# One attention-and-MoE kernel: the first unit's work in one written order, constants in one block, keys in blocks of 32

## The chip, the cores and the metric

The kernel runs on one core of a Trainium2 chip. The metric is the device time of one execution in microseconds (us); the kernel before takes 814.76 us (median of 3 runs, 812.94 to 815.05).

A core has a matrix engine (TensorE: PE for the multiplications, PEld for the loading of their stationary operand), a vector engine (VectorE, DVE), an activation engine (ScalarE, ACT), GpSimd (POOL) and SyncE (SP). Each engine works through its own queue in order and waits on semaphores of the others. Transfers (DMA) are issued from the queue of SP or POOL.

## What is computed

Three layers follow each other, on 2304 tokens (batch 4, sequence 576, 8 heads of 64):

```python
scores = scale * np.matmul(q, k.transpose(0, 1, 3, 2))
rel = pos[:, None] - pos[None, :]
mask_plain = (rel >= 0) & (rel < 32)                      # heads 0 to 3
mask_dil = (rel >= 0) & (rel < 128) & (rel % 4 == 0)      # heads 4 to 7
scores = np.where(mask, scores, -1e9)
attn = np.exp(scores - scores.max(-1)); attn = attn / (attn.sum(-1) + 1e-9)
x = attn @ v                                              # 2304 x 512
h = np.maximum(np.maximum(x @ w1, x @ w2), x @ w3)        # d_ff 768
x = h @ w_out                                             # 2304 x 512
h = x @ w_in                                              # d_ff 2048
g = (a0 + a1*h + a2*h*h + a3*h*h*h) / (1 + |b0|*|h| + |b1|*h*h + 1e-6)
out = g @ w_out2
```

The weights arrive as 64-bit floats.

## The kernel before

**Stages.** The attention and the first MoE are worked through in 6 units of 384 tokens; a unit has 2 chunks of 192 tokens (chunks 0 to 11, three to a batch). Behind the last unit the second MoE runs over 6 tiles of 384 tokens (from about 420 us on).

**Attention of a chunk** has a plain half `p` (heads 0 to 3) and a dilated half `d` (heads 4 to 7). Its steps are: `S` scores (PE, lines 278 and 287; in chunks 0 to 3 PE adds the mask as a product with an identity), `MX` row maximum (DVE, line 307), `E` exponential (ACT, line 318, one instruction a block with a sum in chunks 0 to 3, one for all blocks behind them), `SB` division by the sum (DVE, lines 328 to 330), `X` transposes (PE, line 343) with a copy out of PSUM (ACT line 347 or DVE line 345), `V` product with the values (PE, lines 363 and 369), `VE` the split of the result into a rounded high part `x1h` (ACT, line 384) and a low part `x1l` (DVE, line 385).

**First MoE of a unit** (`moe1`): 18 groups of 12 matmuls of 384 columns (lines 497 to 499: high by high, high by low, low by high), each group's result copied by ACT (line 514) or joined by DVE's maximum (line 516), with a split of the maximum (lines 520, 521), then 4 groups of 18 matmuls whose results go to DRAM (`x2d`) by POOL's queue (line 531).

**Weights of the first MoE** are 18 blocks `w1r` and 6 blocks of `w_out` of 512 KB. Each takes five steps: `load` (SP), `abs` (ACT, line 450), `bits` (two on DVE, lines 456 and 458), `hi` (ACT, line 472), `lo` (DVE, line 480). The second MoE's weights are converted later and stored as `w2d` by POOL's queue (line 478), at a pace tied to PE's progress.

**Order.** The text `START` is a list of words that is issued exactly as written: chunks 0 and 1, a few conversion steps, and `W:n`, n matmuls of 512 columns whose result nobody reads (`warmth`, line 604). Behind it a scheduler of the language orders the instructions by data and priority: unit 0's `moe1` with the conversions and the attention of chunks 2 and 3 (`UNIT0`), then each later unit's `moe1` with the attention of the next (`UNIT`). Loads of queries, keys and values stand on SP's queue.

Of the kernel before, what the change touches and what calls it, by code (L numbers as in the profile page):

```python
# [31 lines left out]

START = """
W:7
S0:p v:0 L:3 S0:d MX0:p E0:p MX0:d S1:p W:2
SB0:p E0:d X0:p,0,1 X0:p,1,1 W:1 MX1:p V0:p SB0:d abs VE0:p bits E1:p S1:d abs X0:d,0,1 W:2 MX1:d X0:d,1,1 W:3 V0:d E1:d W:2 SB1:p VE0:d hi abs lo v:1 L:3
X1:p,0 W:2 SB1:d X1:p,1 bits W:3 V1:p hi W:2 VE1:p lo bits
X1:d,0 W:2 X1:d,1 W:3 V1:d VE1:d hi lo abs
"""

UNIT0 = """
Sa:p
MXa:p Ea:p SBa:p
-
Xa:p,1 Sa:d MXa:d Ea:d SBa:d
-
-
Xa:p,0 Va:p Xa:d,0
VEa:p Xa:d,1
-  # L50
Va:d
VEa:d
-
Sb:p
MXb:p Eb:p
Sb:d MXb:d SBb:p Eb:d Xb:p,0
SBb:d Xb:p,1 Xb:d,0
-
Xb:d,1 Vb:d Vb:p VEb:d
VEb:p  # L60
-
-
-
# [29 lines left out]
def kernel(  # L93
    ctx: ExitStack,
    tc: tile.TileContext,
    masks: bass.AP,
# [10 lines left out]
    a_co: bass.AP,  # L107
    b_co: bass.AP,
# [40 lines left out]
    AHEAD = 1  # L149
# [38 lines left out]
    at_k = {}  # L188
    x1 = {}

    def load_k(b, part=None):

        if b not in at_k:
            at_k[b] = (
                at.tile([128, 2, S], F32, tag="kTp", bufs=2, name=f"kTp{b}"),
                at.tile([128, 8, S // 4], F32, tag="kTd", bufs=2, name=f"kTd{b}"),
            )
        kTp, kTd = at_k[b]
        src = kp_in[b].rearrange("p (a t) -> p a t", a=2)
        if part is None:  # L200
            nc.sync.dma_start(out=kTp, in_=src)
        elif part == 0:
            nc.sync.dma_start(out=kTp[:, :, 0:CH], in_=src[:, :, 0:CH])
            return
        else:
            nc.sync.dma_start(out=kTp[:, :, CH:S], in_=src[:, :, CH:S])
            return
        nc.sync.dma_start(out=kTd.rearrange("p n m -> p (n m)"), in_=kd_in[b])

    def load_q(c, g):  # L210
        if c >= NCH:
            return
        if g == "p":
            t = at.tile([128, 2 * BP, 2 * QP], F32, tag="qTp", bufs=QA, name=f"qTp{c}")
            nc.sync.dma_start(out=t.rearrange("p n w -> p (n w)"), in_=qp_in[c])
        else:
            t = at.tile([128, 8, 2 * M], F32, tag="qTd", bufs=QA, name=f"qTd{c}")
            nc.sync.dma_start(out=t.rearrange("p n w -> p (n w)"), in_=qd_in[c])
        at_raw[c, g] = t
# [8 lines left out]
    def load_v(c):  # L228
        ci = c % NC
        vp = at.tile([WP, BP, NP, D], F32, tag="vp", name=f"vp{c}")  # L230
        nc.sync.dma_start(out=vp.rearrange("p i h d -> p (i h d)"), in_=vp_in[c])
        nm = dil(ci)[1]
        vd = at.tile([WD, NP, 4 * D], F32, tag="vd", name=f"vd{c}")
        nc.sync.dma_start(out=vd[:nm].rearrange("p h e -> p (h e)"), in_=vd_in[c, 0:nm, :])
        at_raw[c, "v"] = (vp, vd)

    def attn_pieces(c):
# [12 lines left out]
        def SC(g):  # L250
# [6 lines left out]
            for j in range(2):  # L257
                at_bank = SC_AT.get((c, g), "sc")
                if at_bank != "sc":
                    t = (mm_p if at_bank == "mm" else pv_p).tile(  # L260
                        [128, 512], F32, tag=at_bank, name="sc")
                else:
                    t = sc_p.tile([128, 512], F32, tag="sc", bufs=2, name="sc")
# [11 lines left out]
            m16, m32 = (mP16, mP32) if plain else (mD16, mD32)  # L275
# [4 lines left out]
            for n in range(U):  # L280
                i, blk = divmod(n, BP)
                if plain:
                    k0 = key0(ci, blk)
                    lq, rk = qT[:, n, :], kTp[:, i, k0:k0 + WP]
                else:
                    lq, rk = qT[:, n, :], kTd[:, n, m0:m0 + nmk]
                nc.tensor.matmul(scs[n // G][:, n % G, :], lhsT=lq, rhs=rk,  # L287
                                 start=not pem, stop=not pem or n % G == G - 1)
            load_q(c + QA, g)
            if g == "d" and ci == 0 and b + 1 < B:  # L290
                load_k(b + 1)
            sb = at.tile([Q, U, WP if plain else WD], F32, tag="s" + g, bufs=SBB, name="sb")
            mx = at.tile([Q, U, 1], F32, tag="mx" + g, bufs=2, name="mx")
            sm = at.tile([Q, U, 1], F32, tag="sm" + g, bufs=2, name="sm")
            grp[g] = (sb[:, :, :W], Q, W, U, sm, mx, scs, mask(m32))

        def MX(g):
# [11 lines left out]
            if c < ACT_UNITS:  # L309
                nc.vector.tensor_scalar_mul(mx, mx, -SCALE)  # L310

        def E(g):
            sv, Q, W, U, sm, mx, scs, mk = grp[g]
            G = U // 2
            if c < ACT_UNITS:
                for n in range(U):
                    src = scs[n // G][:, n % G, :] if c < MASK_PE else sv[:, n]
                    nc.scalar.activation(out=sv[:, n], in_=src, func=AF.Exp, scale=SCALE,
                                         bias=mx[:, n], accum_out=sm[:, n])
            else:  # L320
                nc.vector.tensor_tensor(out=sv, in0=sv, in1=mx.to_broadcast([Q, U, W]),
                                        op=ALU.subtract)
# [3 lines left out]
        def SB(g):  # L326
# [3 lines left out]
            nc.vector.tensor_tensor(out=sv, in0=sv, in1=sm.to_broadcast([Q, U, W]), op=ALU.mult)  # L330

        def X(g, j, dve=False, bank="tp"):
            sv, Q, W, U = grp[g][:4]
            G = U // 2
            if bank == "tp":
                tp = tp_p.tile([128, TU], F32, tag="tp", name="tpp")
            else:
                tp = sc_p.tile([128, 512], F32, tag="sc", bufs=2, name="tpp")[:, 0:TU]
            tp = tp[:W].rearrange("w (n q) -> w n q", q=Q)
            pt = at.tile([WP, TU], F32, tag="pt", bufs=PT, name="pt")[:W].rearrange(  # L340
                "w (n q) -> w n q", q=Q)
# [8 lines left out]
        def V(g):  # L350
            vp, vd = at_raw[c, "v"]
            if c == 0:
                pv = mm_p.tile([128, 512], F32, tag="mm", name="pv")
            else:
                pv = pv_p.tile([128, 512], F32, tag="pv", name="pv")
            pv = pv[:, 0:TU].rearrange("p (a t) -> p a t", a=2)
            for a in range(2):
                pt = pts["p", a] if g == "p" else None
                for n in range(BP if g == "p" else 4):
                    for j in range(2):  # L360
# [6 lines left out]
                        else:  # L367
                            pt = pts["d", j]
                            nc.tensor.matmul(pv[rows, a, M * n:M * n + M],  # L369
                                             lhsT=vd[:nmk, 2 * a + j, D * n:D * n + D],  # L370
                                             rhs=pt[:, 2 * (n // 2) + a,
                                                    M * (n % 2):M * (n % 2) + M],
# [3 lines left out]
        def VE(g):  # L376
            pv = grp["v" + g]
            if g == "p":
                src, dh, dl = pv, x1h[:, 0:2, tok], x1l[:, 0:2, tok]
            else:  # L380
# [65 lines left out]
    def cv_abs(i):  # L446
# [27 lines left out]
    def cv_lo(i):  # L474
# [4 lines left out]
        else:  # L479
            nc.vector.tensor_sub(slot[:, 512:1024], t, slot[:, 0:512].bitcast(F32))  # L480

    cv_at = {"load": 0, "abs": 0, "bits": 0, "hi": 0, "lo": 0}
    cv_steps = (("hi", cv_hi, "bits"), ("lo", cv_lo, "bits"), ("abs", cv_abs, "load"),
                ("bits", cv_bits, "abs"), ("load", cv_load, None))

# [15 lines left out]

    def moe1(u):
        x1h, x1l = x1[u]
        hs = {}
        for f in range(F1):
            for j in range(3):
                ps = mm_p.tile([128, 512], F32, tag="mm", name="mm")
                o = ps[:, 0:TU]
                w = w1s[f, j]
                mm3(o, [(w[:, 128 * c:128 * c + 128], w[:, 512 + 128 * c:640 + 128 * c],  # L510
                         x1h[:, c, :], x1l[:, c, :]) for c in range(KC)])
                if j == 0:
                    t = com.tile([128, TU], F32, tag="m", bufs=MB, name="m")
                    nc.scalar.activation(out=t, in_=o, func=AF.Copy)
                else:
                    nc.vector.tensor_tensor(out=t, in0=o, in1=t, op=ALU.max)  # L516
                if j == 2:
                    hh = com.tile([128, TU], F32R, tag=f"hh{f}", name=f"hh{f}")
# [386 lines left out]
```

## Time and profile before

| | us |
|---|---|
| median of 3 runs | 814.76 |
| the profiled execution | 815.14 |
| its span, first to last instruction | 813.4 |

The profile was taken from one execution. Its page gives busy times and the chain of work that ended last; its trace can be asked for stretches, single lines, tiles and rows in order of time. Times in rows are counted from the span's start. A busy PE is not PE at its peak: matmuls overlap, so the pace is read from start to start. PEclk is the granted TensorE clock, 1.00 for 2.4 GHz and 0.50 for 1.2 GHz.

### The profile page before, as it was taken

To read this page: it belongs to the slowest core of one execution; us is meant where nothing else is said; L and a number is where in the kernel's file an instruction comes from. 1 tells how busy PE (TensorE), PEld (TensorE's weight loads), DVE (VectorE), ACT (ScalarE), POOL (GpSimd) and SP (SyncE) were. 2 spreads that over 40 slices of the span, in tenths; PEclk is the share of its full clock that TensorE was granted. 3 is DMA by queue.
4 is the path that set the end of the run, shared out by engine and by line. 5 is a ranking of instruction groups with operands and counts; after the bars stand their busy time and mean duration, and the time that the engine had idled before them with its cause. 6 is when DMAs were issued, how large, how long until landed. Compare 5 with 4: busy or idle time off the path is not lost.

```text
span 813.4 us, 13081 instructions
## 1 busy us (share of the span) xinstructions
PE 800.1 (98%) x4965; PEld 745.1 (92%) x4965; DVE 614.1 (76%) x1184; ACT 487.9 (60%) x1023; POOL 39.2 (5%) x77
## 2 busy tenths in 40 slices
PE   7899999999999999999999999999999999999998
PEld 5699999999999999999998899999999999999996
DVE  2679755655656646637389899999999999998996
ACT  3578623333333334245398887787778778777775
POOL 0000000110111110000000000000000000000000
PEclk9799999999999999999999999999999999999999
DMA  8677435754554544328310011010002001001001
GB/s 267 245 263 271 159 106 171 228 167 158 171 175 161 178 163 149 107 101 272 120 63 1 1 39 40 1 42 37 1 1 79 1 0 40 1 1 38 2 1 39
DMA packets 29438, 82.54 MB, mean 101 GB/s; under 512 B 3904, under 2 KB 7488, under 8 KB 29376
## 3 DMA queue, kind: packets, MB, share of 16 engines
q1 hardware_dynamic: 24080, 64.66, 24.7%
q0 software_dynamic: 5296, 17.04, 5.5%
q8 instruction: 39, 0.64, 0.3%
q14 instruction: 23, 0.19, 0.1%
HBM read 63.87 MB, written 17.83 MB: 100 GB/s over the span
## 4 chain that ended last, share of the span: by engine, by line
PE 96%; ACT 1%; DVE 1%; DMA 1%; issue 0%; SPq 0%; POOL 0%; ACTq 0%
PE mm L498 12%; PE mm L497 12%; PE mm L499 12%; PE h L498 8%; PE acc L769 8%; PE h L499 8%; PE h L497 8%; PE acc L767 8%; PE acc L768 8%; PE sc L287 4%; PE tpp L343 2%; PE pv L369 2%; PE pv L363 1%; DMA mk<-in_masks_dram 1%; ACT x1h L384 1%; PE warmth L604 0%
## 5 line engine op out<-in xcount | busy, mean ns | idle before, releaser
L497 PE MATMUL mm<-x1h,w1s 128*128 128x384 f32 x432 | 147.7, 343 | 0.0
L498 PE MATMUL mm<-x1l,w1s 128*128 128x384 f32 x432 | 146.0, 338 | 1.0 <-DVE x1l L385 1.0
L499 PE MATMUL mm<-x1h,w1s 128*128 128x384 f32 x432 | 145.2, 336 | 0.0
L498 PE MATMUL h<-x2l,w2s 128*128 128x384 f32 x384 | 129.2, 337 | 0.0
L499 PE MATMUL h<-x2h,w2s 128*128 128x384 f32 x384 | 129.0, 336 | 0.0
L497 PE MATMUL h<-x2h,w2s 128*128 128x384 f32 x384 | 128.9, 336 | 0.0
L767 PE MATMUL acc<-w2s,gh 128*128 128x512 f32 x288 | 113.6, 395 | 0.0
L768 PE MATMUL acc<-w2s,gh 128*128 128x512 f32 x288 | 113.4, 394 | 0.0
L769 PE MATMUL acc<-w2s,gl 128*128 128x512 f32 x288 | 109.8, 395 | 0.0
L718 ACT ACTIVATE q<-h 128x384 f32<-128x384 f32 x96 | 47.2, 491 | 76.1 <-PE h L499 75.5
L498 PEld LDWEIGHTS mm<-x1l,w1s 128*128 128x128 f32 x432 | 81.6, 189 | 2.2 <-DVE x1l L385 2.2
L497 PEld LDWEIGHTS mm<-x1h,w1s 128*128 128x128 f32 x432 | 81.3, 189 | 0.6
L499 PEld LDWEIGHTS mm<-x1h,w1s 128*128 128x128 f32 x432 | 81.6, 189 | 0.0
L497 PEld LDWEIGHTS h<-x2h,w2s 128*128 128x128 f32 x384 | 72.1, 188 | 3.9
L498 PEld LDWEIGHTS h<-x2l,w2s 128*128 128x128 f32 x384 | 72.0, 188 | 3.8
L499 PEld LDWEIGHTS h<-x2h,w2s 128*128 128x128 f32 x384 | 72.1, 188 | 0.3
L516 DVE TENSOR_TENSOR m<-mm,m 128x384 f32<-128x384 f32 x72 | 39.9, 554 | 42.2 <-PE mm L499 41.4
L725 DVE SCALAR_TENSOR_TENSOR q<-q,cs,ab 128x384 f32<-128x384 f32 x96 | 59.1, 615 | 15.5 <-ACT ab L719 15.4
L720 ACT ACTIVATE p<-h,cs 128x384 f32<-128x384 f32 x96 | 65.1, 678 | 0.0
L769 PEld LDWEIGHTS acc<-w2s,gl 128*128 128x128 f32 x288 | 54.1, 188 | 11.9
L768 PEld LDWEIGHTS acc<-w2s,gh 128*128 128x128 f32 x288 | 54.1, 188 | 9.4
L767 PEld LDWEIGHTS acc<-w2s,gh 128*128 128x128 f32 x288 | 54.0, 188 | 9.0
(86 smaller groups left out, 1471.8 us busy)
## 6 DMA issues: line engine op xcount, KB each, us to landing
w1r<-in_w_dram SPq DMA_DIRECT2D x18, 512.0 KB, 6.6
raw<-in_w_in_dram SPq DMA_DIRECT2D x16, 512.0 KB, 4.0
w2d<-cvt POOLq DMA_DIRECT2D x32, 256.0 KB, 2.6
raw<-in_w_out_dram SPq DMA_DIRECT2D x16, 512.0 KB, 3.6
w2r<-w2d SPq DMA_DIRECT2D x32, 256.0 KB, 3.6
qTp<-in_qp_dram SPq DMA_DIRECT2D x12, 384.0 KB, 4.1
qTd<-in_qd_dram SPq DMA_DIRECT2D x12, 384.0 KB, 4.5
x2d<-xs POOLq DMA_DIRECT2D x24, 192.0 KB, 2.5
```

The lines of the kernel that those rows point to most:

```text
L287: nc.tensor.matmul(scs[n // G][:, n % G, :], lhsT=lq, rhs=rk, start=not pem, stop=not pem or n % G == G - 1)
L343: nc.tensor.transpose(tp[:, i, :], sv[:, G * j + i, :], ident[:Q, :Q])
L497: nc.tensor.matmul(o, lhsT=lh, rhs=rh, start=(i == 0), stop=False)
L498: nc.tensor.matmul(o, lhsT=lh, rhs=rl, start=False, stop=False)
L499: pe_at[0] = nc.tensor.matmul(o, lhsT=ll, rhs=rh, start=False, stop=(i == n - 1))
L516: nc.vector.tensor_tensor(out=t, in0=o, in1=t, op=ALU.max)
L718: nc.scalar.activation(out=s["q"], in_=s["h"], func=AF.Square)
L720: nc.scalar.activation(out=s["p"], in_=s["h"], func=AF.Identity, scale=cs[:, 3:4], bias=cs[:, 2:3])
L725: nc.vector.scalar_tensor_tensor(out=s["q"], in0=s["q"], scalar=cs[:, 5:6], in1=s["ab"], op0=ALU.mult, op1=ALU.add)
L767: nc.tensor.matmul(o, lhsT=gh, rhs=w[:, 0:512], start=(c == 0), stop=False)
L768: nc.tensor.matmul(o, lhsT=gh, rhs=w[:, 512:1024], start=False, stop=False)
L769: nc.tensor.matmul(o, lhsT=gl, rhs=w[:, 0:512], start=False, stop=(c == F2 - 1))
```

## The change

The written order `START` now holds all of unit 0: the attention of chunks 0 to 3, all 24 weight conversions and all of unit 0's `moe1`, so that the scheduler begins with unit 1's `moe1`. The word for the conversion's first step is now `up`. New words: `H:j` is group j of `moe1` on the first 192 columns, `P:n` group n on the rest or on all columns, `M`, `HH`, `HL`, `Y`, `YS` the steps behind a group. `W:n` no longer issues matmuls of 512 columns but 4n of 128 columns, in the bank that the next step takes. `E` is one of three kinds in chunks 0 to 3 (`A` with sums by ACT, `C` block by block with the sum by DVE, `B` one instruction for all blocks), and the division may be done by ACT (`SB0:p,act`).

The two masks and the identity come in 16 bits in the same block as the coefficients (`consts`), so that two casts and the two small coefficient loads go. Plain keys lie in blocks of 32 tokens, first the one half of the heads, then the other. The tokens of a chunk are ordered by their rest modulo 4 within 64, and the host puts the output's rows back; so the split of a dilated result reads and writes rows without a stride, and the `V` matmul of the dilated half writes three runs of 16. Loads of queries, keys and values behind the start go to POOL's queue.

```diff
-W:7
-S0:p v:0 L:3 S0:d MX0:p E0:p MX0:d S1:p W:2
...
+qp0 kp0 mk L W:19 S0:p,mm qd0 kd0 up MX0:p bits L E0:p qd1 hi W:10 S0:d,mm SM0:p L up lo
+SB0:p,act MX0:d W:1 S1:d,sc qp1 D0:d bits kp1 E0:d X0:p,0,mm up X0:p,1,mm SM0:d v0 XC0:p,0 MX1:d
...
+    EXPS = {"0:p": "C", "1:d": "A", "2:p": "A", "2:d": "A", "3:p": "C", "3:d": "C"}
...
+    def keep_warm(t):
+        for _ in range(4 * idle[0]):
+            nc.tensor.matmul(t[:, 384:512], lhsT=warm, rhs=warm, start=True, stop=True)
+        idle[0] = 0
+        return t
...
+        queue = nc.sync if b < 2 else nc.gpsimd        # load_k
+        queue = nc.sync if c < 2 * QA else nc.gpsimd   # load_q
+        queue = nc.sync if c < 4 else nc.gpsimd        # load_v
...
-                    lq, rk = qT[:, n, :], kTp[:, i, k0:k0 + WP]
+                    lq, rk = qT[:, n, :], kTp[:, k0 // 32:(k0 + WP) // 32, i, :]
...
-                            nc.tensor.matmul(pv[rows, a, M * n:M * n + M],
-                                             lhsT=vd[:nmk, 2 * a + j, D * n:D * n + D],
+                            at_n = pv[rows, a].rearrange("p (i r m) -> p r i m", r=4, m=16)[:, n]
+                            nc.tensor.matmul(at_n, lhsT=vd[:nmk, 2 * a + j, D * n:D * n + D],
...
-                src = pv.rearrange("p a (r m) -> p a r m", r=4)
-                dh = x1h[:, 2:4, tok].rearrange("p a (m r) -> p a r m", r=4)
-                dl = x1l[:, 2:4, tok].rearrange("p a (m r) -> p a r m", r=4)
+            return pv, x1h[:, at_p, tok], x1l[:, at_p, tok]
...
+                elif op == "H":
+                    m1_mm(0, 0, int(arg), slice(0, CH))
+                elif op == "P":
+                    f, j = divmod(int(arg), 3)
+                    m1_mm(0, f, j, slice(CH if (0, f, j) in m1 else 0, TU))
...
-        for u in range(NU):
+        for u in range(1, NU):
```

What stood on PE ahead of the first group of `moe1` before: an unread matmul, the last `V` of chunk 1, then three matmuls of 384 columns that repeat with the next weights.

```order
L604 LDWEIGHTS warm
L604 MATMUL warmth<-warm 128x512
L369 MATMUL pv<-pt,vd_389 64x48 x16
L497 MATMUL mm<-x1h_172,w1s_0_382 128x384
L498 MATMUL mm<-x1l_173,w1s_0_382 128x384
L499 MATMUL mm<-x1h_172,w1s_0_382 128x384
```

And on PE now (`vd_373` and `vd_421` are the values of chunks 0 and 1, `spare` holds chunk 1's probabilities):

```order
L376 MATMUL tpp<-mk,spare 80x96 x8
L407 MATMUL pv<-pt,vd_373 64x3x16 x16
L407 MATMUL pv<-pt,vd_421 64x3x16 x16
L376 MATMUL tpp<-mk,spare 96x128 x6
L537 MATMUL mm<-x1h_150,w1s_0_261 128x192
L538 MATMUL mm<-x1l_151,w1s_0_261 128x192
L539 MATMUL mm<-x1h_150,w1s_0_261 128x192
```

The first group now stands ahead of chunk 1's plain `V`, on 192 columns, without an unread matmul near it.

DVE at the start of the program before (L307 maximum, L328 to L330 division, L345 copy behind a transpose):

```order
L584 CAST mP_158<-mk 128x288
L307 TENSOR_REDUCE mx<-sc 128x3 x2
L310 TENSOR_SCALAR mx<-mx 128x6
L307 TENSOR_REDUCE mx<-sc 96x4 x2
L310 TENSOR_SCALAR mx<-mx 96x8
L328 TENSOR_SCALAR sm<-sm 128x6
L329 RECIPROCAL sm<-sm 128x6
L330 TENSOR_TENSOR sb<-sb,sm 128x576
L624 TENSOR_SCALAR cs<-co 128x4
L345 COPY pt<-tpp 96x384
```

And now (L323 maximum, L496, L498 and L520 conversion of the first weight block, L358 sum, L339 difference):

```order
L323 TENSOR_REDUCE mx<-sc 128x3 x2
L326 TENSOR_SCALAR mx<-mx 128x6
L496 TENSOR_SCALAR cvt<-cvt 128x512
L498 SCALAR_TENSOR_TENSOR cvt<-w1r_0_147,cvt 128x512
L358 TENSOR_REDUCE sm<-sb 128x6
L520 TENSOR_TENSOR w1s_0_261<-cvt,w1s_0_261 128x512
L362 TENSOR_SCALAR sm<-sm 128x6
L363 RECIPROCAL sm<-sm 128x6
L323 TENSOR_REDUCE mx<-sc 96x4 x2
L339 TENSOR_TENSOR sb<-sc,mx 96x4x48 x2
```

The conversions of weights now stand between the steps of chunk 0 from the first maximum on; before, the first stood 20 instructions further down.

POOL's queue in unit 1 before holds stores alone:

```order
L531 DMA x2d<-xs 128x384 x4
L478 DMA w2d_103<-cvt 128x512
L478 DMA w2d_104<-cvt 128x512
L478 DMA w2d_105<-cvt 128x512
L478 DMA w2d_106<-cvt 128x512
```

And now (`vp_1798` and `vd_1800` are the values of chunk 5, `qTp_1791` the queries of chunk 7):

```order
L592 DMA x2d<-xs 128x384
L218 DMA qTp_1487<-in_qp_dram 128x768
L221 DMA qTd_1564<-in_qd_dram 128x768
L518 DMA w2d_103<-cvt 128x512
L518 DMA w2d_104<-cvt 128x512
L238 DMA vp_1798<-in_vp_dram 96x768
L518 DMA w2d_105<-cvt 128x512
L241 DMA vd_1800<-in_vd_dram 80x1024
L518 DMA w2d_106<-cvt 128x512
L218 DMA qTp_1791<-in_qp_dram 128x768
```

Loads of values and queries now stand between the stores and behind what these wait for.

## Rows read from the trace of the kernel before

**Rows 1.** The page: shares of the chain that ended last, by engine.

```profile
PE 96%; ACT 1%; DVE 1%; DMA 1%; issue 0%; SPq 0%; POOL 0%; ACTq 0%
```

**Rows 2.** Two stretches: busy us of PE, PEld, DVE, ACT, POOL (x instructions), PEclk, DMA, GB/s.

```profile
8.00:41.80 33.80, 30.32 (x250) 24.14 (x250) 18.49 (x49) 17.17 (x80) 0.39 (x2) 0.84 0.77 259
41.80:105.20 63.40, 63.40 (x470) 61.05 (x469) 50.26 (x104) 44.84 (x115) 1.76 (x3) 0.98 0.64 226
```

**Rows 3.** PE in order of time: start us, us from first start to last end.

```profile
8.64 2.71 PE L287 MATMUL sc<-kTp,qTp 128*128 128x96 f32 x12
...
30.14 0.53 PE L343 MATMUL tpp<-mk,sb 128*96 128x128 f32 x3 [1.87 <-ACT pt L347]
...
41.82 0.69 PE L497 MATMUL mm<-x1h,w1s 128*128 128x384 f32 x1
...
44.80 0.34 PE L497 MATMUL mm<-x1h,w1s 128*128 128x384 f32 x1
...
105.22 0.33 PE L497 MATMUL mm<-x1h,w1s 128*128 128x384 f32 x1
...
109.20 0.34 PE L499 MATMUL mm<-x1h,w1s 128*128 128x384 f32 x1
```

**Rows 4.** Single microseconds of PE: length, busy us (x instructions), PEclk, DMA, GB/s.

```profile
31.00:32.00 1.00, 0.44 (x2) 0.53 1.00 401
...
44.00:45.00 1.00, 1.00 (x6) 0.64 0.97 320
```

**Rows 5.** PE in order of time: a plain V, a plain S and what follows it.

```profile
61.04 0.92 PE L363 MATMUL pv<-pt,vp 96*64 96x64 f32 x24
...
75.03 1.47 PE L287 MATMUL sc<-kTp,qTp 128*128 128x96 f32 x12
76.29 0.42 PE L497 MATMUL mm<-x1h,w1s 128*128 128x384 f32 x1
```

**Rows 6.** DVE's groups from 0 to 105 us: busy us, mean ns, idle before.

```profile
L480 DVE TENSOR_TENSOR w1s<-cvt,w1s 128x512 fp32r<-128x512 f32 x18 | 12.3, 681 | 0.0
L458 DVE SCALAR_TENSOR_TENSOR cvt<-w1r,cvt 128x512 int32<-128x512 int32 x18 | 12.2, 684 | 0.2
L456 DVE TENSOR_SCALAR cvt<-cvt 128x512 int32<-128x512 int32 x24 | 9.7, 418 | 0.0
...
L307 DVE TENSOR_REDUCE mx<-sc 128x3 f32<-128x288 f32 x8 | 3.4, 449 | 2.9 <-PE sc L287 2.9
...
L330 DVE TENSOR_TENSOR sb<-sb,sm 128x576 f32<-128x576 f32 x4 | 3.0, 755 | 0.1
L307 DVE TENSOR_REDUCE mx<-sc 96x4 f32<-96x320 f32 x4 | 1.8, 480 | 2.0 <-PE sc L287 2.0
...
L330 DVE TENSOR_TENSOR sb<-sb,sm 96x384 f32<-96x384 f32 x2 | 1.1, 551 | 0.0
...
L329 DVE RECIPROCAL sm<-sm 96x8 f32<-96x8 f32 x4 | 0.8, 194 | 0.1
```

**Rows 7.** One of four hand-overs between units, in order of time (DVE, PE).

```profile
168.54 0.85 DVE L385 TENSOR_TENSOR x1l<-pv,x1h 128x384 fp32r<-128x384 f32 x1 [0.76 <-ACT x1h L384]
...
168.88 0.34 PE L497 MATMUL mm<-x1h,w1s 128*128 128x384 f32 x1
...
169.45 0.44 PE L498 MATMUL mm<-x1l,w1s 128*128 128x384 f32 x1 [0.24 <-DVE x1l L385]
```

**Rows 8.** Waits of the whole span: us in total, times, longest us.

```profile
POOL w2d L478 <- DVE cvt L458: 163.1, 27, 12.6
...
PEld mm L498 <- DVE x1l L385: 2.2, 4, 0.6
```

**Rows 9.** The chain in order of time: start us, us, what.

```profile
2.08 5.57 DMA mk<-in_masks_dram
```

**Rows 10.** The DMA view from 0 to 60 us.

```profile
DMA packets 5341, 15.33 MB, mean 255 GB/s; under 512 B 843, under 2 KB 1355, under 8 KB 5336
```

**Rows 11.** The tile `w2d` from 100 to 420 us, stores from POOL's queue.

```profile
DMA to landing us min/median/max: 2.3/3.2/6.2
```

More of the change, by code (lines that the diff above doesn't have):

```diff
@@ L95 @@
     tc: tile.TileContext,
-    masks: bass.AP,
+    consts: bass.AP,
     kp_in: bass.AP,
@@ L188, with bank @@
     at_k = {}
+    done_v = {}
+    idle = [0]
+    def keep_warm(t):
[3 more added lines that the diff above has]
+        return t
+    def bank(pool, name):
+        if pool == "tp":
+            t = tp_p.tile([128, 512], F32, tag="tp", name=name)
+        elif pool == "sc":
+            t = sc_p.tile([128, 512], F32, tag="sc", bufs=2, name=name)
+        else:
+            t = (mm_p if pool == "mm" else pv_p).tile([128, 512], F32, tag=pool, name=name)
+        return keep_warm(t)
     x1 = {}
+    spare = []
     def load_k(b, part=None):
@@ L198, in load_k @@
         kTp, kTd = at_k[b]
[L199 to L208, printed above, removed]
+        queue = nc.sync if b < 2 else nc.gpsimd
+        for k, cut in ((0, slice(0, CH // 32)), (2, slice(CH // 32, S // 32))):
+            if part in (None, k):
+                queue.dma_start(out=kTp[:, cut].rearrange("p n a t -> p (n a t)"),
+                                in_=kp_in[b][:, 64 * cut.start:64 * cut.stop])
+        if part in (None, 1):
+            queue.dma_start(out=kTd.rearrange("p n m -> p (n m)"), in_=kd_in[b])
     def load_q(c, g):
@@ L257, in SC @@
             for j in range(2):
[L258 to L263, printed above, removed]
+                t = bank(pool, "sc")
                 ww = WP if plain else WD
@@ L273, in mask @@
                 return mk[:, i:i + 1, :W].to_broadcast([Q, G, W])
-            m16, m32 = (mP16, mP32) if plain else (mD16, mD32)
+            m16 = mP16 if plain else mD16
             if pem:
@@ L308, in MX, with DF @@
                                             axis=AX.X, op=ALU.max)
-            if c < ACT_UNITS:
+            if mode[g] != "B":
                 nc.vector.tensor_scalar_mul(mx, mx, -SCALE)
+        def DF(g):
+            sv, Q, W, U, sm, mx, scs, mk = grp[g]
+            G = U // 2
+            if mode[g] != "B":
+                return
+            if c >= MASK_PE:
+                nc.vector.tensor_tensor(out=sv, in0=sv, in1=mx.to_broadcast([Q, U, W]),
+                                        op=ALU.subtract)
+            else:
+                for j in range(2):
+                    h = slice(j * G, j * G + G)
+                    nc.vector.tensor_tensor(out=sv[:, h], in0=scs[j],
+                                            in1=mx[:, h].to_broadcast([Q, G, W]),
+                                            op=ALU.subtract)
         def E(g):
@@ L499, in mm3, with m1_mm, m1_max @@
             pe_at[0] = nc.tensor.matmul(o, lhsT=ll, rhs=rh, start=False, stop=(i == n - 1))
+    m1 = {}
+    def m1_mm(u, f, j, cols=slice(0, TU)):
+        if (u, f, j) not in m1:
+            m1[u, f, j] = bank("mm", "mm")[:, 0:TU]
+        x1h, x1l = x1[u]
+        w = w1s[f, j]
+        mm3(m1[u, f, j][:, cols], [(w[:, 128 * c:128 * c + 128], w[:, 512 + 128 * c:640 + 128 * c],
+                                    x1h[:, c, cols], x1l[:, c, cols]) for c in range(KC)])
+    def m1_max(u, f, j):
+        o = m1[u, f, j]
+        if j == 0:
+            m1[u, f] = com.tile([128, TU], F32, tag="m", bufs=MB, name="m")
+            nc.scalar.activation(out=m1[u, f], in_=o, func=AF.Copy)
+        else:
+            nc.vector.tensor_tensor(out=m1[u, f], in0=o, in1=m1[u, f], op=ALU.max)
@@ L596, in cv_step @@
             cv_at[name] += 1
-        def busy(n, bank="mm"):
-            if bank == "mm":
-                t = mm_p.tile([128, 512], F32, tag="mm", name="warmth")
-            else:
-                t = sc_p.tile([128, 512], F32, tag="sc", bufs=2, name="warmth")
-            for _ in range(n):
-                nc.tensor.matmul(t, lhsT=warm[:, 0:128], rhs=warm[:, 0:512], start=True, stop=True)
         with tc.manual_schedule():
@@ L609 @@
                 if op == "L":
-                    for _ in range(int(arg)):
-                        cv_step("load")
-                elif op == "v":
-                    load_v(int(arg))
+                    cv_step("load")
+                elif op in loads:
+                    loads[op]()
                 elif op == "W":
-                    busy(*[x if x.isalpha() else int(x) for x in arg.split(",")])
+                    idle[0] = int(arg)
+                elif op == "H":
[3 more added lines that the diff above has]
+                    m1_mm(0, f, j, slice(CH if (0, f, j) in m1 else 0, TU))
+                elif op == "M":
+                    m1_max(0, *divmod(int(arg), 3))
+                elif op in ("HH", "HL", "Y", "YS"):
+                    {"HH": m1_hh, "HL": m1_hl, "Y": m1_y, "YS": m1_ys}[op](0, int(arg))
                 elif op in steps:
@@ L619 @@
                     do(word)
-                    done_words.add(word)
         cs = const.tile([128, 8], F32, name="cs")
@@ L628 @@
         nc.vector.memset(cs[:, 7:8], -64.0 * LN2)
+        assert not cv
+        cv_es[0].close()
+        cv_es[0] = ExitStack()
+        cv_p[0] = cv_es[0].enter_context(
+            tc.tile_pool(name="cv2", bufs=1, side="right", reuse_waits="tile"))
+        for c in (4, 5):
+            for g in "pd":
+                load_q(c, g)
+        load_k(2)
         tick = 0
-        for u in range(NU):
+        for u in range(1, NU):
             last = u == NU - 1
@@ L661 @@
                 slot += 1
-                if u == 0:
-                    pass
-                elif not last:
+                if not last:
                     tick += 1
```

300 lines of the change are left out of this document (148 added, 152 removed).

## Prediction, made before the changed kernel ran

> **What bounds the kernel now.** I read the chain of work that ended last first: 96% of it is PE [rows 1]. So a change counts by what it does to PE's own time: how early PE gets dense work, what it waits for in between, and at which clock it runs. Then I cut the span at two points of PE's order of time: the first matmul of unit 0's first MoE at 41.82 us and the first of unit 1's at 105.22 us [rows 3]. Behind the second cut the changed kernel does the same work in the same kind of order, so what it gains ahead of the cut moves the end by as much.
>
> In the stretch from 8 to 41.8 us nothing is full: PE has an instruction in flight for 30.3 of 33.8 us, but DVE works for only 18.5 and ACT for 17.2, and the granted clock is 0.84 on average [rows 2]. The chain there goes from engine to engine through chunks 0 and 1. In the stretch from 41.8 to 105.2 PE is busy throughout, DVE for 50.3 and ACT for 44.8 of 63.4 us [rows 2]. The matmuls of 384 columns follow each other every 173 ns (24 of them from 105.22 to 109.20, 23 steps in 3.98 us [rows 3]); the 288 of unit 0 are thus 50 us, the rest is attention of chunks 2 and 3.
>
> The clock: it fell to 0.5 in the microsecond from 31 on, behind a pause of 1.87 us on PE, and came back between 44 and 45 us, some 2.8 us after the stream of 384-column matmuls had begun [rows 3, 4]. At the very start it was low too: 12 score passes took 2.71 us at 8.64, and 1.47 us at 75.03 [rows 3, 5].
>
> **The change, part by part.** First the point at which the dense stream starts. Behind it PE has written work without a gap, ahead of it DVE has the longest queue: up to the low part of chunk 0's dilated result, which the first half group needs, the order lists 3 `bits` pairs, 2 `lo`, 8 maxima, 4 differences, 3 sums, 3 divisions, 2 `VL` and 10 small ones. With DVE's mean times [rows 6]: 3 x (0.418 + 0.684) + 2 x 0.681 = 4.7; maxima 4 x 0.449 + 4 x 0.480 at most = 3.7; differences, not shown before, read the same PSUM tiles, 4 x 0.48 = 1.9; sums, bounded by the division of the same width, 3 x 0.755 = 2.3; divisions 0.551 + 0.755 + 0.84 (0.755 by the width of 640) = 2.1; `VL` 2 x 0.551 = 1.1; small ones 10 x 0.194 at most = 1.9. Together 17.7 us.
>
> It begins when the first score bank is full. The block of constants landed at 7.65 us [rows 9]; it stays third in SP's queue and gets smaller, and the casts that stood behind it go. The first bank is half a plain `S`, 0.6 us at full clock (12 passes from 75.03 to 76.29 [rows 5]) and a mask: 8.6 us. Without any wait of DVE the stream starts at 8.6 + 17.7 = 26.3 us. With DVE as full as it was in the second stretch, 50.26 / 63.4 = 79% [rows 2], it is 8.6 + 22.4 = 31.0. I take 28.5, nearer to the dense end: conversions now stand between the attention steps as filling, and ACT has fewer microseconds ahead of that point than DVE. So the stream starts 13.3 us earlier than at 41.82.
>
> Second, what the stream has to hold. It was 63.4 us. Into it come pieces that stood ahead of it: the plain `V` of chunk 1, 0.9 [rows 5]; the plain `S` of chunk 2, 1.3 of passes [rows 5] and two masks, 0.2; half of the dilated `S` of chunk 2, 0.9 by the same pace of 105 ns a pass. Three groups are cut into halves of 192 columns, 36 matmuls more: at the least what a matmul takes beyond its columns, 173 - 384 / 2.4 = 13 ns, so 0.5 us; at the most 105 ns for each of the 72 halves, the pace of a pass with 96 columns and the same 128 columns of weights [rows 5], so 7.6 - 6.2 = 1.3. I take 0.7. I leave the cost of the low clock at its head in: 9 matmuls took 2.98 us from 41.82 to 44.80 instead of 1.56 [rows 3], 1.4 us, because the order has only 16 unread matmuls between chunk 1's dilated scores and the stream. Sum: 63.4 + 0.9 + 1.5 + 0.9 + 0.7 = 67.4. The end of unit 0 then lies at 28.5 + 67.4 = 95.9 instead of 105.2: **9.3 us gained**.
>
> Does that hold for the other engines? DVE did 18.5 + 50.3 = 68.8 us from 8 to 105 [rows 2]; sums and differences add about 4.2 (5 sums, 4 differences), four divisions that move to ACT take 2.9 away and the rows without stride some 1.2. That is 69 of 87 us. ACT gets 28 division blocks on its 62 us [rows 2]. Transfers: the start's list is 20.6 MB; at the mean of 255 GB/s [rows 10] the last block lands at about 81 us, and is used by the last groups, from about 85 on. All three just fit, none has much to spare.
>
> Third, the hand-over between later units. There PE waits for the low part of the dilated result, four times, 2.2 us of waits [rows 8]. Of one, PE's loss is what lies between 168.88 + 0.17 and 169.45 [rows 7], 0.4 us. Its split loses the stride and takes 0.55 as the plain halves do [rows 6] instead of 0.85 [rows 7], on ACT and on DVE each, so it ends about 0.6 earlier: the wait goes, and nothing else is late there. 4 x 0.4 = **1.6 us**.
>
> Edits that I cost at nothing: the values' product with three runs of 16 and the keys in blocks of 32 (same columns; bounds: nothing below, and above 12 plain `S` of 1.3 us slower by a tenth, 1.6 us); the coefficients, which were loaded far ahead of their use. The loads that move to POOL: each takes a place behind stores that wait for DVE, 163.1 us in 27 waits, 12.6 at the longest [rows 8], and lands 2.3 to 6.2 us after its issue [rows 11]. Behind a waiting store stand the next chunk's values, for which `V` waits. One `V` is about 25 us ahead of the next (half of a unit of some 63 us as in the second stretch [rows 2], less the steps that have to stand between), so 12.6 + 6.2 = 18.8 us is covered.
>
> The stores from POOL's queue landed in 3.2 us in the median and 6.2 at the most [rows 11], with DVE at work on the next conversions. The Trainium skill warns here (SBUF — State Buffer, section "SBUF: two separate sides"): descriptors of a transfer from GpSimd's queue cannot be written while DVE runs an instruction in a two-port mode, so such a transfer starts late. By that rule the moved loads would be late by single DVE instructions, under 1 us each, and the sum would not change; it would count only where the cover of rival 4 is used up.
>
> **The sum.** The profiled execution took 815.14 us, 0.38 above the median. 815.14 - 9.3 - 1.6 = 804.2, less 0.38: **803.9 us**.
>
> **Rivals.** 1. The clock stays at 1.2 GHz through the whole first phase, as it did from 8.64 us on before, since scores, transposes and `V` did not raise it between 32 and 44 us although PE was busy [rows 2, 3, 4]. For it: unread matmuls of 512 columns at the start did not help before. Against it: now 76 stand there and 40 more behind the first scores, and the clock was full before the pause at 30 us. Price: first bank 1 us, the last transposes and two `V` on the chain some 2, and plain `V` and `S` in the stream's head 2: 5 us, so 809.
>
> 2. DVE holds PE back inside the stream. Ahead of the last group of four output groups (4 x 18 x 0.173 = 12.5 us on PE, and some 2.5 of attention) DVE must have done about 64.5 of its 69 us; the forecast asks for 64.5 / (80.9 - 8.6) = 89%. At 85% the point moves to 8.6 + 75.9 = 84.5, the end of unit 0 to 99.5: 3.6 us lost, 807.5.
>
> 3. The change does not do what it says: loads of weights stand ahead of the dilated queries and keys in SP's queue, chunks 0 and 1 wait for data, and the stream starts where it did. Then only the hand-overs remain, less the longer stream: 814 to 815.
>
> 4. Slower than before: the loads of values on POOL's queue. If they start more than 18.8 us late, each of the 8 later chunks makes PE wait. It decides at 25 us; to lose the 10.9 us gained and 2.4 more, each of 8 has to be 1.7 us beyond its cover: 817.5. Against it: the longest wait seen in that queue is 12.6 us [rows 8].
>
> **How the numbers follow.** A measurement of this kernel can tell about 0.3%, 2.4 us, from no change. Forecast 0.68 (799.5 to 806.5: its low end is a start at 26.3 and a stream at full clock, 92.3, which gives 800.3), rival 1 0.12, rival 2 0.11, rival 3 0.05, rival 4 0.04. Rivals 1 and 2 lie below 812.3, so faster is 0.91, within 0.3% 0.05, slower 0.04. The range for 8 in 10 reaches over rivals 1 and 2: 799.5 to 809.5. Its upper end also holds a start at 31 with halves at 1.3 us.
>
> **What would show it.** Right: the first matmul of 192 columns between 26 and 31 us; the first of unit 1 between 92 and 100; DVE over 85% busy between; no wait of PE for the low part at the four hand-overs; from there to the end the same length as before less 1.6 us. Rival 1 shows as a granted clock of 0.5 from 10 to 28 us; rival 2 as waits of PE or its weight loads for DVE's `lo` or for a bank that a maximum holds; rival 4 as PE waiting for a transfer at a `V`. Wrong: a stream that starts past 33 us, or PE idle by more than 3 us inside it.

## The result, and the profile after

The changed kernel takes **803.93 us** (median of 4 executions, 799.41 to 807.06); the kernel before, beside it on the same chip, 814.62. The ratio is 0.9863, its 95% interval 0.9835 to 0.989: 10.7 us, 1.4%, faster. The forecast was 803.9. Its sum was wrong in two places that cancelled, as the traces below show.

The profiled execution is the slowest of the four, 807.06 us with a span of 805.3. The shares of its chain, beside [rows 1]:

```profile
PE 90%; DVE 4%; ACT 3%; DMA 2%; issue 1%; SPq 1%; ACTq 0%; DVEq 0%
```

PE's share fell from 96% to 90%. Before, the chain stayed on PE from 41.8 to 105.2 us. Now it runs through steps of DVE and ACT from 43 us until a group of transposes on PE, which waited for a division on DVE:

```profile
91.61 0.51 PE L376 MATMUL tpp<-mk,sb 128*96 128x128 f32 x3 [0.80 <-DVE sb L365]
```

So inside unit 0 PE is no longer the only limit, although it stands still for only 1.2 of 73.4 us there. Now the stretches of [rows 2], cut at the first matmul of 192 columns and at unit 1's first, then four pieces of 5 us (length, busy us of PE, PEld, DVE, ACT and POOL with counts, PEclk, DMA share, GB/s):

```profile
8.00:29.30 21.30, 19.64 (x236) 18.26 (x236) 16.97 (x42) 15.06 (x47) 0.00 (x0) 0.76 1.04 323
29.30:102.70 73.40, 72.19 (x554) 69.25 (x553) 53.40 (x111) 48.29 (x133) 6.71 (x12) 0.93 0.62 213
...
15.00:20.00 5.00, 3.34 (x32) 2.89 (x30) 4.07 (x12) 4.19 (x20) 0.00 (x0) 0.92 1.06 174
20.00:25.00 5.00, 5.00 (x55) 4.32 (x54) 3.40 (x9) 3.08 (x7) 0.00 (x0) 0.50 1.03 297
35.00:40.00 5.00, 5.00 (x26) 4.87 (x26) 3.07 (x6) 1.90 (x5) 0.00 (x0) 0.53 1.03 405
40.00:45.00 5.00, 5.00 (x47) 4.98 (x47) 4.00 (x9) 4.39 (x18) 1.37 (x2) 1.00 1.05 328
```

PEclk is the row to read: TensorE ran at its lower level, 1.2 GHz, from about 20 to 40 us, so some 10 us of the stream of `moe1` ran at half pace too. Before it fell, PE had waited 1.49 us for the rest of the keys. PE in order of time, beside [rows 3]:

```profile
18.07 1.83 PE L297 MATMUL sc<-kTp,qTp 128*128 128x96 f32 x12 [1.49 <-DMA kTp<-in_kp_dram]
...
29.35 0.51 PE L537 MATMUL mm<-x1h,w1s 128*128 128x192 f32 x1
```

```profile
102.73 0.33 PE L537 MATMUL mm<-x1h,w1s 128*128 128x384 f32 x1
```

The stream starts 12.5 us earlier than at 41.82, but unit 1 starts only 2.5 us earlier than at 105.22. Yet the span is 8.1 us shorter. The rest came behind the point from which, by the prediction, almost nothing should change. From unit 1's first matmul to the first `h` matmul of the second MoE (which stands at 407.0 us before, not at about 420): 301.8 us before, 299.6 after. From there to the end: 813.4 - 407.0 = 406.4 before, 805.3 - 402.3 = 403.0 after. In this last stretch PE does not wait before, and once, for 0.4 us, after; its matmuls follow each other faster: the matmul behind one with `gl` starts after 233 ns on average before and after 227 now. The second MoE, the tile `h` (count, duration, first and last start) and the groups of 512 columns from 450 to 790 us (count, busy us, mean ns of one), before:

```profile
L497 PE MATMUL h<-x2h,w2s x384: 334/334/342, 407.0 to 800.5; 128*128 128x384 f32 x192
...
L767 PE MATMUL acc<-w2s,gh 128*128 128x512 f32 x246 | 97.1, 395 | 0.0
L768 PE MATMUL acc<-w2s,gh 128*128 128x512 f32 x245 | 96.5, 394 | 0.0
L769 PE MATMUL acc<-w2s,gl 128*128 128x512 f32 x245 | 95.3, 395 | 0.0
```

and after:

```profile
L537 PE MATMUL h<-x2h,w2s x384: 332/334/346, 402.3 to 792.6; 128*128 128x384 f32 x192
...
L817 PE MATMUL acc<-w2s,gh 128*128 128x512 f32 x246 | 96.6, 393 | 0.0
L816 PE MATMUL acc<-w2s,gh 128*128 128x512 f32 x246 | 96.2, 391 | 0.0
L818 PE MATMUL acc<-w2s,gl 128*128 128x512 f32 x247 | 94.8, 389 | 0.0
```

Two questions follow: what spreads the changed kernel over 8 us, and what makes the second MoE shorter with the same instructions.

### The profile page after: what moved, and what is told of

Its sections match the earlier page's. It is cut to its first block, busy times and chain, and to the rows that moved or that the text cites. A ratio compares the mean times of both kernels' runs of the same rounds, so it can differ in the third digit from the quotient of the medians.

```text
span 805.3 us, 13363 instructions
## 1 busy us (share of the span) xinstructions
PE 797.5 (99%) x5108; PEld 753.0 (94%) x5108; DVE 612.6 (76%) x1184; ACT 486.4 (60%) x1007; POOL 59.3 (7%) x113
## 4 chain that ended last, share of the span: by engine, by line
PE 90%; DVE 4%; ACT 3%; DMA 2%; issue 1%; SPq 1%; ACTq 0%; DVEq 0%
PE mm L537 11%; PE mm L539 11%; PE mm L538 11%; PE acc L817 8%; PE acc L816 8%; PE acc L818 8%; PE h L539 8%; PE h L537 8%; PE h L538 8%; PE sc L297 3%; PE tpp L376 2%; PE pv L407 1%; DMA kTp<-in_kp_dram 1%; PE pv L399 1%; DVE cvt L498 1%
## 5 line engine op out<-in xcount | busy, mean ns | idle before, releaser
L537 PE MATMUL mm<-x1h,w1s 128*128 128x384 f32 (+1 forms) x444 | 151.8, 343 | 0.0
L539 PE MATMUL mm<-x1h,w1s 128*128 128x384 f32 (+1 forms) x444 | 148.9, 335 | 0.0
L538 PE MATMUL mm<-x1l,w1s 128*128 128x384 f32 (+1 forms) x444 | 148.8, 335 | 0.0
L818 PE MATMUL acc<-w2s,gl 128*128 128x512 f32 x288 | 108.1, 389 | 0.0
L537 PEld LDWEIGHTS mm<-x1h,w1s 128*128 128x128 f32 x444 | 84.9, 192 | 0.7
L538 PEld LDWEIGHTS mm<-x1l,w1s 128*128 128x128 f32 x444 | 85.3, 192 | 0.0
L539 PEld LDWEIGHTS mm<-x1h,w1s 128*128 128x128 f32 x444 | 85.1, 192 | 0.0
```

The costliest lines, as they stand in the source:

```text
L537: nc.tensor.matmul(o, lhsT=lh, rhs=rh, start=(i == 0), stop=False)
L538: nc.tensor.matmul(o, lhsT=lh, rhs=rl, start=False, stop=False)
L539: pe_at[0] = nc.tensor.matmul(o, lhsT=ll, rhs=rh, start=False, stop=(i == n - 1))
L818: nc.tensor.matmul(o, lhsT=gl, rhs=w[:, 0:512], start=False, stop=(c == F2 - 1))
```

## Experiments on the spread

**The changed kernel again** (`a0_again`), no edit.

> The changed kernel once more, nothing edited. Theory C (the clock): its times fall into two groups, 799 to 802 us at a mean granted clock of 0.997 and 805 to 808 at 0.987, since in some executions TensorE is granted its lower level from 20 to 40 us; a trace of the upper clock has unit 1's first matmul at 96 to 97 us, one of the lower clock near 102.7. Rival D (the transfers): the spread is that of the DMA, so a trace with the keys late has unit 1 late whatever the clock. For the 3.4 us that the second MoE took less in the first trace (403.0 against 406.4): if the layout of the constants did that, it is 403 again; if it varies from one execution to another, it is not.

Measured: 805.77 us, 799.62 to 810.14. The ten executions of both series, with the mean granted clock of each:

| us | 799.41 | 799.62 | 801.91 | 802.57 | 804.28 | 805.96 | 807.06 | 807.26 | 807.41 | 810.14 |
|---|---|---|---|---|---|---|---|---|---|---|
| clock | 0.997 | 1.000 | 0.998 | 0.995 | 0.990 | 0.988 | 0.987 | 0.987 | 0.987 | 0.985 |

The profiled one is now that of 799.62 us. The same pieces of its first phase, then PE in order of time:

```profile
15.00:20.00 5.00, 2.75 (x31) 2.46 (x30) 3.67 (x10) 3.67 (x19) 0.00 (x0) 1.00 1.06 182
20.00:25.00 5.00, 4.87 (x109) 4.22 (x107) 4.70 (x12) 3.41 (x8) 0.00 (x0) 1.00 1.02 304
```

```profile
18.54 1.55 PE L297 MATMUL sc<-kTp,qTp 128*128 128x96 f32 x12 [2.25 <-DMA kTp<-in_kp_dram]
...
26.17 0.33 PE L537 MATMUL mm<-x1h,w1s 128*128 128x192 f32 x1
```

```profile
95.63 0.33 PE L537 MATMUL mm<-x1h,w1s 128*128 128x384 f32 x1
```

The keys came later than in the first trace, the clock stayed at its upper level, and unit 1 starts at 95.63 (96 to 97 were expected) instead of 102.73. Rival D falls: the keys were later and unit 1 was earlier, so the 7.1 us go with the clock. But the pause alone is not its switch either: 2.25 us here without a fall, 1.49 us there with one. The second MoE is again 797.8 - 395.2 = 402.6.

**More unread matmuls** (`a1_fill`), 40 in the place of 12 ahead of chunk 1's plain scores:

```diff
-XC0:p,1 SB0:d W:3 S1:p,mm
+XC0:p,1 SB0:d W:10 S1:p,mm
```

> 28 more unread matmuls (40 instead of 12) ahead of chunk 1's plain scores, 60 ns each, so that PE has some 1.7 us more to do where it waited 1.49 us for the keys. Theory C: the clock holds at 1.00 from 15 to 45 us in most executions, mean clock 0.997, 799 to 802 us in nearly all of them. Rival D: the wait was no cause of the clock; the fillers cost up to 1.7 us, 804 to 806 median with the same spread.

Measured: **799.67 us** (798.45 to 800.68), ratio to the kernel before 0.9816, interval 0.9801 to 0.983, with mean clocks of 0.997 to 1.000 in all four. PE's pause ahead of the scores has gone (its row carries no wait), and the clock was low for some 3.5 us only (0.96 and 0.69 of two pieces of 5 us):

```profile
20.00:25.00 5.00, 4.37 (x87) 3.87 (x85) 4.78 (x11) 3.34 (x8) 0.00 (x0) 0.96 1.01 373
25.00:30.00 5.00, 5.00 (x49) 4.76 (x48) 3.65 (x8) 4.03 (x9) 0.00 (x0) 0.69 1.04 401
```

```profile
17.16 1.55 PE L297 MATMUL sc<-kTp,qTp 128*128 128x96 f32 x12
...
24.95 0.51 PE L537 MATMUL mm<-x1h,w1s 128*128 128x192 f32 x1
```

This is the best version of the study, 4 to 6 us under the changed kernel's two medians, and the base of the experiments below that say so. With these fillers 17 of the 20 timed executions of it and of the kernels built on it had a mean clock of 0.997 or more; without them 3 of 10.

**Keys ahead of weights** (`a2_keys`): `qp1` ahead of the second block of weights, `kp1` ahead of the third.

> The two loads for chunk 1's plain scores (queries, rest of the keys) are issued ahead of one and two blocks of weights. Rival D: the 1.49 us wait for the keys goes, and with it that much and the spread, 800 to 802 us. Theory C: the wait goes, but the clock decides; if the wait set off the low clock 799 to 802, if the thin matmuls from 18 to 29 us did, 804 to 806 with the clock down from about 20 us.

Measured: 804.8 us (801.67 to 805.8). The wait for the keys went, and two others came, 0.57 us for the dilated queries, now behind these loads, and this one:

```profile
19.73 0.28 PE L285 MATMUL sc<-mk 128*128 128x288 bf16 x1 [2.27 <-ACT pt L387]
```

In its trace the clock is 0.53 from 20 to 25 us. Rival D falls once more, but since PE paused elsewhere, the run doesn't tell the pause from the thin matmuls as the cause.

**No unread matmuls** (`a3_nofill`): every `W:n` out of `START`.

> All 148 unread matmuls of the first phase are left out. Theory C: the clock is at the lower level through most of the first 40 us, mean clock 0.98 to 0.985 in every execution, and unit 1's first matmul at 103 to 106 us: 807 to 811 us. Rival D: the first scores begin up to 2 us sooner and nothing else changes: 801 to 804.

Measured: 804.47 us (801.45 to 805.38), so theory C was wrong in size: as the changed kernel places them, the fillers (136; the 148 above is my miscount) earn nothing that shows. In the trace the clock fell at 25 us, not in the first 20, and came back in the piece from 35 to 40:

```profile
20.00:25.00 5.00, 3.77 (x77) 3.09 (x75) 4.10 (x10) 4.66 (x18) 0.00 (x0) 1.00 1.02 309
25.00:30.00 5.00, 4.91 (x48) 4.70 (x49) 4.83 (x11) 3.94 (x8) 0.00 (x0) 0.55 1.02 401
30.00:35.00 5.00, 5.00 (x41) 4.71 (x41) 2.50 (x6) 2.28 (x4) 0.00 (x0) 0.50 1.04 405
```

So it is shown that the clock makes most of the spread (not all: 801.91 us at 0.998 stands beside 799.41 at 0.997) and that more unread matmuls in front of the keys hold the clock in most executions. What exactly sets off its fall between 20 and 25 us isn't settled.

## Experiments on the parts

**The order of tokens alone** (`b1_order`), in the kernel before: masks, plain queries and output rows permuted, the dilated `V` product written in three runs of 16, and

```diff
-                src = pv.rearrange("p a (r m) -> p a r m", r=4)
-                dh = x1h[:, 2:4, tok].rearrange("p a (m r) -> p a r m", r=4)
-                dl = x1l[:, 2:4, tok].rearrange("p a (m r) -> p a r m", r=4)
+            src, dh, dl = pv, x1h[:, at_p, tok], x1l[:, at_p, tok]
```

> The kernel before with the order of tokens alone: the 64 tokens of a block stand by rest modulo 4 (masks, plain queries and the output's rows permuted, dilated probabilities times values written in that order), so that both copies of the dilated half run on contiguous columns. Theory O (the prediction's): the four waits of 0.2 to 0.3 us for x1l at the units' starts go, and some of the time around them, 1.0 to 1.6 us in all: 813 to 813.8 us; the second MoE stays at 406.4. Rival A: nothing that can be measured, the units' gain is that of the addresses: 814 to 815 us.

Measured: 811.2 us (810.51 to 812.93), ratio 0.9959 (0.995 to 0.9969): 3.7 us, more than expected. A hand-over in its trace, beside [rows 7]:

```profile
165.77 0.62 PE L493 MATMUL mm<-x1h,w1s 128*128 128x384 f32 x2
166.23 0.35 PE L494 MATMUL mm<-x1l,w1s 128*128 128x384 f32 x1
```

```profile
166.40 0.56 DVE L381 TENSOR_TENSOR x1l<-pv,x1h 128x384 fp32r<-128x384 f32 x1 [0.40 <-ACT x1h L380]
```

The low part takes 0.56 us instead of 0.85, and no row of PE carries a wait there. Units 1 to 5 take 299.7 us instead of 301.8, just as in the changed kernel (299.6), so the order of tokens alone gives these 2.1 to 2.2 us. The other 1.5 to 1.8 are unit 0's (unit 1 starts at 103.44 in the place of 105.22): in this trace the clock was back at 40 us, in those of the kernel before, `b2_pad` and `b3_pad96` at 44 to 45. Whether the order of tokens does that isn't settled.

**The place of the tiles.** Constants stand first in SBUF, and the tiles `x1h`, `x1l`, `m`, `hh`, `hl`, later `gh`, `gl` and nine of the 32 `w2s` behind them. With smaller constants all of these moved, and with them the first MoE's weights and the work tiles of ACT and DVE, which lie on the same side: by the program's allocation they begin at byte 20032 of a partition before and at 18848 after. (The difference, 1184 bytes, is that of the constants' sizes in the two kernels; no trace shows the first bytes themselves.) Five kernels move these tiles and nothing else, by a few bytes that nobody uses: `b2_pad` and `b3_pad96` from the kernel before, `c1_pad`, `c3_pad64` and `c2_pad128` from `a1_fill`:

```diff
-        co = const.tile([128, 6], F32, name="co")
+        co = const.tile([128, 14], F32, name="co")    # b2_pad; 30 in b3_pad96
...
-        cs = const.tile([128, 8], F32, name="cs")
+        cs = const.tile([128, 16], F32, name="cs")    # c1_pad; 24 in c3_pad64, 40 in c2_pad128
```

> The kernel before with nothing edited but the place of its tiles: 32 bytes more behind the coefficients move everything that is allocated on the left side of SBUF behind the constants (x1h, x1l, m, hh, hl, and later gh, gl and the last w2s) by 32 bytes, from multiples of 64 to multiples of 64 plus 32, where the changed kernel has them. Theory A (addresses): the second MoE takes 402.6 us from its first h matmul to the end, as in all five traces of the changed kernel so far, instead of 406.4, and units 1 to 5 some tenths less each: 809 to 811 us. Rival I (the instructions): the place makes no difference, 814 to 815 us and 406.4.

> The changed kernel with 40 fillers ahead of chunk 1's plain scores (799.7 us) and 32 bytes more behind the constants, which moves the same tiles to multiples of 64, where the kernel before has them. Theory A: the second MoE takes 406.4 us again and units 1 to 5 somewhat longer: 803.5 to 805.5 us. Rival I: 799 to 801 us, with 402.6 for the second MoE.

> The changed kernel with 40 fillers ahead of chunk 1's plain scores (799.7 us) and 128 bytes more behind the constants. So far the second MoE took 402.6 us with the left side's tiles at 32 (modulo 128), 405.7 at 64, and in the kernel before 406.4 at 64 and 406.1 at 96. Theory P (the place within 128 bytes decides): 32 again, so 402.6 us, 799 to 801 us in all. Rival Q (the 32 bytes took it away by something else, as the distance to other tiles): 404 to 406 for the second MoE, 801 to 805 us.

> The same with 64 bytes more in the place of 128, so that the left side's tiles lie at 96 (modulo 128). Theory P: slow as the kernel before was at 96, 405.5 to 406.5 us for the second MoE, 802.5 to 805 us in all. Rival P64 (the place within 64 bytes, and something else in the kernel before): 402.6.

> The kernel before with 96 bytes more behind the coefficients, so that the left side's tiles lie at 32 (modulo 128), where the changed kernel has them. Theory P: the second MoE takes 402.6 us in the place of 406.4, 811 us in all. Rival Q: 406 and 814.5 us, the place within 128 bytes is not what the two kernels differ by.

Measured (the second MoE from its first `h` matmul to the end of the span):

| kernel | first byte | modulo 256 | second MoE | time |
|---|---|---|---|---|
| before, `b1_order` | 20032 | 64 | 406.4, 406.4 | 814.62, 811.2 |
| `b2_pad` | 20064 | 96 | 406.1 | 814.52 |
| `b3_pad96` | 20128 | 160 | 402.8 | 811.33 |
| after and `a` kernels, 7 traces | 18848 | 160 | 402.6 to 403.0 | |
| `c1_pad` | 18880 | 192 | 405.7 | 804.33 |
| `c3_pad64` | 18912 | 224 | 405.7 | 803.97 |
| `c2_pad128` | 18976 | 32 | 405.5 | 804.28 |

`c1_pad` settles that the place decides: 32 bytes give back 3.1 us (405.7 for the 402.6 of `a1_fill`). The chip it ran on doesn't explain it: `a6_whole` ran on that of `c1_pad` and `a5_sp` on that of the other two `c` kernels, with 402.6 and 402.8. `b3_pad96` settles the other side: 96 unused bytes make the kernel before 3.4 us faster (ratio 0.9956, 0.9941 to 0.9971) with the changed kernel's pace. The `h` tile (span 802.0) and the `gl` group of `c1_pad`:

```profile
L537 PE MATMUL h<-x2h,w2s x384: 333/334/346, 396.3 to 789.3; 128*128 128x384 f32 x192
...
L818 PE MATMUL acc<-w2s,gl 128*128 128x512 f32 x243 | 94.8, 394 | 0.0
```

and of `b3_pad96` (span 809.8):

```profile
L497 PE MATMUL h<-x2h,w2s x384: 332/334/346, 407.0 to 797.0; 128*128 128x384 f32 x192
...
L769 PE MATMUL acc<-w2s,gl 128*128 128x512 f32 x247 | 94.5, 389 | 0.0
```

The theories of a period of 64 and of 128 bytes both fell (`b2_pad`, `c2_pad128`). A period of 256 fits all 14 traces, 160 with the shorter time and the five others with the longer, but it was formed on them and not tried on a new kernel; 0 and 128 weren't tried. All tiles of the side moved together, so the runs don't tell which of them does it. The units of the first MoE do not care: 62.3 us in `c1_pad` as in `a1_fill`. (The whole times of the three `c` kernels lie 4.3 to 4.7 us above `a1_fill`, since their first phases were later as well: unit 1 at 96.8 to 97.1 us in their traces, against 95.04. PE waited 0.3 to 0.9 us for the keys there, and in `c2_pad128` and `c3_pad64` 1.9 and 1.7 us more ahead of two mask products, at 53 and 79 us; why isn't settled.) The Trainium skill (SBUF — State Buffer, section "SBUF: two separate sides") says that on the engines' side only the port pair of GpSimd and VectorE contends and that PE waits for nobody; the traces show PE's pace change with the place of tiles in that memory, and what inside the memory does it, they don't show.

**Whole groups** (`a6_whole`), on `a1_fill`: the words `H:0`, `H:1`, `H:2` out of `START`, so that `P:0` to `P:2` take all columns.

> The changed kernel with 40 fillers ahead of chunk 1's plain scores (799.7 us), where the first three groups of unit 0 run on all 384 columns at once behind chunk 1's values instead of on two halves of 192. Theory S (the split pays): without it PE has nothing to do while chunk 1's probabilities are turned round and multiplied, and its stream begins 2 to 4 us later, of which it gets back 1.75 us for 36 long matmuls of 174 ns in the place of 72 short ones of 111: 800.5 to 802.5 us. Rival N: the halves' overhead eats what they start earlier, 799 to 800.

Measured: 802.48 us (801.17 to 805.98) against 799.67. PE now waits for chunk 1's split:

```profile
28.22 0.94 PE L399 MATMUL pv<-pt,vp 96*64 96x64 f32 x24 [0.37 <-ACT pt L387]
30.01 0.44 PE L537 MATMUL mm<-x1h,w1s 128*128 128x384 f32 x1 [0.84 <-ACT x1h L419]
31.11 0.44 PE L538 MATMUL mm<-x1l,w1s 128*128 128x384 f32 x1 [0.66 <-DVE x1l L423]
```

From chunk 1's plain scores (19.97) to unit 1's first matmul (97.96) it took 78.0 us, against 77.1 in `a0_again` and 76.4 in `a5_sp`, all at the upper clock. That is 0.9 to 1.6 us for the split; but `c3_pad64` and `c2_pad128`, which have the split, took 77.8 and 78.9 at the upper clock, so these traces don't tell what it is worth. By the medians it is 2.8 us, with two of the four executions at mean clocks of 0.994 and 0.989; the two at 0.997 and 1.000 took 801.17 and 801.95. So theory S has its time, and the two waits of 0.84 and 0.66 us are what is shown of its mechanism.

**Loads on SP** (`a5_sp`), on `a1_fill`: `queue = nc.sync` in all three loaders.

> The changed kernel with 40 fillers ahead of chunk 1's plain scores (799.7 us), where queries, keys and values of chunks 4 and later are issued by SP again in the place of POOL. Theory N: units 1 to 6 wait for no load by either queue: 799 to 801 us, the units 62.3 to 62.5 us each as now. Rival W (the prediction's fourth, that POOL's waits for conversions make these loads late): SP's loads are sooner and the units shorter by some tenths, 797 to 799. Rival L: on SP they stand behind loads of the second MoE's weights that wait for buffers, and PE waits: 801 to 806.

Measured: 800.1 us (798.99 to 801.01), units 1 to 4 62.3 to 62.5 us each, as in `a1_fill`. Theory N holds: from unit 1 on PE waits for none of these loads on either queue.

## Why the prediction was right in time and wrong in its sum

**What bounds the kernel.** Right, but for one sentence: "Behind the second cut the changed kernel does the same work in the same kind of order, so what it gains ahead of the cut moves the end by as much." It does the same work faster, 3.4 to 3.8 us in the second MoE, because smaller constants moved the tiles. That term was missing. And ahead of the cut PE's own time is no longer the whole of it: unit 0's chain went through DVE and ACT from 43 to 91.6 us (in `a0_again` from 38 to 84.5, behind the transfers of weights), and PE, idle for 1.2 and 1.6 us in its stream, kept pace with it.

**The start of the stream.** 28.5 was predicted: 26.17 at the upper clock, 29.35 with the lower one from 20 us on. Right, within the 26 to 31 that were named.

**What the stream holds.** 67.4 with 1.4 of low clock in it, thus 66.0 without; 69.46 in `a0_again`, where the clock never fell. Two terms were too small. Halves follow each other every 111 ns, so 72 x 0.111 - 36 x 0.174 = 1.7 us in the place of 0.7, above the bound of 1.3. And PE stood idle for 1.6 us, which I had as zero: 0.8 for a division on DVE, 0.4 for a copy, 0.3 for queries. Some 0.8 stays unassigned. The end of unit 0 fits (95.63 for 95.9) only because the start was 2.3 early.

**The clock.** This step failed. I let it be low only at the stream's head, for 1.4 us. It was low from 20 to 40 us in the profiled execution, whose mean of 0.987 half of the ten come near or below, and that cost 7.1 us at unit 1's start: 102.73 there, outside the 92 to 100 that were to show the forecast right. Rival 1 named the mechanism, but put it at 10 to 28 us, at 5 us, and at a chance of 0.12. Its "as it did from 8.64 us on before" was also misread: before, the granted clock was 1.00 in the pieces from 15 to 30 us.

**The hand-overs.** Right in mechanism; 4 x 0.54 = 2.2 us in the place of 1.6.

**The other engines.** DVE was to be over 85% busy in the stream; it was 54.9 of 69.5 us, 79%, in `a0_again`. From 50 to 80 us it was at 91 to 95%, and behind that PE waited 0.8 us for DVE, at 84.5: rival 2's loss came, for a division and not for `lo` or a bank, at 0.8 us in the place of 3.6. Transfers ended by 70 us, not 81, at 325 GB/s instead of 255. Of rival 3 came a wait of 1.5 to 2.3 us for the keys, but the stream still started at 26 to 29 us. Rival 4 didn't come: `a5_sp` shows it. The sentence on the rule of the Trainium skill (SBUF — State Buffer, section "SBUF: two separate sides") stands as it was weighed: values loaded from POOL's queue landed in 4.0 us in the median, 5.5 at the most, and PE waited for none of them.

**The sum at the upper clock** is 10.2 (unit 1 at 95.04) + 2.2 + 3.8 = 16.2, the span of `a1_fill` under that of before (813.4 - 797.2). In the median execution of the changed kernel about 5 us of it are lost to the clock, by its distance from `a1_fill`. The forecast of 10.9 left out the 3.8 that came and the 5 that went. So the median met the number by luck. What the profile of before gave was the 9.3 and the 1.6, and of these the 9.3 is itself two misses that cancel, the start 2.3 us early and the stream 2.1 us longer.

## What to carry to other kernels

Shortening a phase that hands work from engine to engine is worth what the clock leaves of it: look at PEclk in the stretch, and give PE something to do in front of the transfer that is latest there. Compare stretches that the edit doesn't touch as well; if their pace changed without a wait, look where the edit moved the tiles, and try a few bytes of padding before believing in a cause. Ask also which engine the chain will run through once the stretch is shorter: here it left PE for DVE and ACT. A forecast that meets the time should be checked term by term, since its errors can cancel.

## What the runs showed of the hardware that was not expected

The place of tiles in SBUF changes the pace of PE's matmuls: behind a 512-column matmul with `gl` the next one starts after 227 ns on average at one place and after 231 to 234 at five others, and the stage differs by 0.7 to 0.9%. TensorE's clock fell in one execution behind a pause of 1.49 us and not in another of the same kernel behind 2.25 us. A matmul of 192 columns follows the last one after 111 ns, not after half of the 174 ns of one with 384.
